# Top-32 attention and a routed expert layer on one core: part of the scores computed ahead and kept in DRAM, and a row-sum step given to ScalarE

## The chip, the core and the metric

The kernel runs on one core of a Trainium2 chip. The engines named below are those of the profile: PE is TensorE (matrix products; PEld is its weight load), DVE is VectorE, ACT is ScalarE, POOL is GpSimd, and SP is the engine that issues most of the DMAs. The metric is the device time of one execution in microseconds (us); the number given for a kernel is the median of its runs.

## The reference

What is computed, cut to what matters:

```python
# q, k, v: (8 batches, 8 heads, 576 rows, 64), fp32
scores = scale * (q @ k.T)                        # 576 x 576 for each head
kth    = the 32nd largest score of each row
attn   = softmax of the scores >= kth, all others 0, divided by (row sum + 1e-9)
x      = heads of (attn @ v) side by side         # 4608 tokens x 512

logits = x @ w_gate                               # 8 experts
e      = argmax(logits); gate = its softmax probability
out    = gate * (relu(x @ w1[e]) @ w2[e])         # w1: 512 x 1024, w2: 1024 x 512 for each expert
```

## The kernel before, in words

**Units and turns.** Two heads of one batch make a *unit*: the 128 partitions of its `qkb` tile hold both heads' 64 dimensions. A batch has four units, worked on in two pairs. A 576-row score matrix is cut into four tiles of 128 rows and a tail of 64 rows. `groups` (L229) orders the work of a pair: four groups of two tiles (tile i of both heads) of the first unit, one group of tails (both units), four groups of the second unit. That is 9 *turns* for a pair, 18 for a batch, 144 in all. Batches are counted from 1 here, as in the title; the code counts them from 0.

**One turn** (`loop`, L909) does these things for group i, and each belongs to a fixed engine, in an order written out by hand for PE, ACT and DVE:

- `products` (L263, matmuls L276): PE computes scores into PSUM tiles `sc`, four turns ahead. The four matmuls of a group take the two heads, that is, the lower and the upper 64 partitions, in alternation.
- `scores` (L279, L283): ACT copies them to SBUF, tile `s`, three turns ahead (`AHEAD`). There are four buffers of `s`.
- `fold` and `fold_on` (L290 to L300): DVE folds the scores of group i+1 by maximum and minimum. `search` (L317 to L354): DVE finds the 32nd largest of each row by rounds of MAX8 and MATCH_REPLACE8 (L329 to L345). Its last result goes to `low`, by ACT (L354).
- `depths` (ACT, L370), `less` (POOL, L379) and `weights` (ACT, L387, exponentials with the row sums added up into `z`) make the attention weights `w`.
- `transposed` (PE L398 to L411, ACT L404 to L419) turns the weights of group i-1.

**Endings.** When a unit's tiles are done, `ending` (L804) multiplies by v (`outputs`, L421: PE L432, ACT L434), turns the result back (PE L443, ACT L450), and makes divisors from the row sums (`divisors`, L452). These steps are spread over the following turns: each `yield` of `ending` names a place of the turn (`"products"`, `"relu"`, `"small"` ...) at which `at_place` resumes it. Small DVE steps are put into a list `aside`; `tick` (L304) issues one of them between two instructions of the search. `divisors` consists of three such steps on DVE: the sum plus 1e-9 (L454), its reciprocal (L456), and a copy of 64 values of the last column to other partitions (L458). POOL then multiplies by the divisors (`logits` L466, `rows` L479).

**Expert blocks.** Rows are scattered in DRAM by expert (L546). A *block* of 128 rows of one expert takes 4 MB of weights, two DMAs by SP (L635, L637), and is computed on PE in 16 pieces (`block`, L674: L688 and L703). `pieces` (L773) puts some of them into each turn by a credit that grows by a fixed `rate`; from the 14th turn of a batch on (`FIRST`) the rate is set by the number of blocks that became known with the batch before. The number of pieces put into the turns does not depend on any time. What is left runs after the last turn.

**Queues.** SP carries out its DMAs strictly in the order in which the scheduler placed them: an instruction that waits for a buffer holds all behind it. `load_unit` (L141) brings `qkb` (two buffers), `load_values` (L245) brings v, and the pool `wp` has two buffers each for `w1` and `w2`. POOL's order is placed by the scheduler too.

The functions that the diff touches, and what calls them:

Of the kernel before, what the change touches and what calls it, by code (L numbers as in the profile page):

```python
# [9 lines left out]
F32 = mybir.dt.float32  # L10
I32 = mybir.dt.int32
AF = mybir.ActivationFunctionType
# [9 lines left out]
EPS = 1e-9  # L22
# [13 lines left out]
def kernel(  # L36
# [6 lines left out]
    moe_w2: bass.AP,  # L43
    out: bass.AP,
):

# [36 lines left out]
    nc = tc.nc  # L83
# [6 lines left out]
    NC = 4  # L90
# [103 lines left out]
    for n in range(2):  # L194
        t = const.tile([P, S if n else KC * P], F32, name=f"oT{n}")
        if not n:
            nc.gpsimd.memset(t[:, S:], 0.0)
        oT_of.append(t)
        t = const.tile([P, NT + 1], F32, name=f"rz{n}")
        nc.gpsimd.memset(t, 0.0)  # L200
        rz_of.append(t)
    wT = const.tile([P, NC, 2, S + ST], F32, name="wT")
    wTt = const.tile([P, S + ST], F32, name="wTt")
# [75 lines left out]
    def scores(got):  # L279

        s = k.att.tile([P, 2, 2, HF], F32, name="s", bufs=2 if k.exact else 4)
        return s, [
            lambda m=m, ps=ps: nc.scalar.copy(s[:, m, :, :], ps[:, :, 0:HF]) for m, ps in enumerate(got)  # L283
        ]
# [166 lines left out]

    def divisors(n):  # L452
        rz = rz_of[n.u % 2]
        nc.vector.tensor_scalar_add(rz[:, 0:NT], n.z, EPS)  # L454
        yield
        nc.vector.reciprocal(rz[:, 0:NT], rz[:, 0:NT])  # L456
        yield
        nc.vector.tensor_copy(rz[0:ST, NT:NT + 1], rz[ST:P, NT - 1:NT])  # L458
        yield

    def logits(n, lg):
# [269 lines left out]
    ON_CHIP = 3  # L731
    KEEP = 3 * PIECES
    BETWEEN = 2

    with fast:
        units = [(b, u) for b in range(B) for u in range(U)]
# [67 lines left out]
        def ending(b, u):  # L804

            nonlocal left
            n = unit[b * U + u]
            if u == 0:
                x_of[b] = k.xp.tile([P, KC, XW], F32, name="x")
                in_turn(token_ids(x_of[b][:, :, Dm + 1].bitcast(I32), b))  # L810
                lg_of[b] = k.small.tile([P, KC, E], F32, name="lg")
            x, lg = x_of[b], lg_of[b]
            out_steps = outputs(n, x)
            yield "products"
            next(out_steps)
            if u % 2 == 0:
                yield "relu"
                next(out_steps)
            yield "small"
            div = divisors(n)  # L820
            aside.append(div)
            if u % 2:
                yield "relu"
                next(out_steps)
            yield "products"
            next(out_steps)
            if b * U + u + 2 < len(units):
                load_values(unit[b * U + u + 2])
            yield "relu"
            next(out_steps)  # L830
            yield "products"
            next(out_steps)
            yield "relu"
            next(out_steps, None)
            yield "rows"
            through(div)
            logits(n, lg)
            rows(n, x)
            if u < U - 1:
                return  # L840
            yield "small"
            r = choice(lg)
            aside.append(r.steps)
            yield "weights"
            yield "turn"
            through(r.steps)
            nc.scalar.activation(lg, lg, AF.Exp)
            yield "products"
            ranks(r)
            yield "small"  # L850
            steps = places(r, x)
# [12 lines left out]
            new = LAST - SURE if b == B - 1 else new_of[b]  # L864
            if new:
                slot_i = slot_last if b == B - 1 else k.small.tile([1, 2, NSLOT], I32, name="slot_i")
                steps = table(slot_i, new, b == B - 1)
                aside.append(steps)
                yield "weights"
                yield "pool"  # L870
                yield "weights"
                yield "pool"
                through(steps)
                coming.extend((slot_i[0:1, 0, j:j + 1], slot_i[0:1, 1, j:j + 1]) for j in range(new))
            if b == B - 1:
                spare.extend(coming[ALWAYS - SURE:])
                del coming[ALWAYS - SURE:]
                assert len(loaded) == 2 and not waiting
                fill_up()
                coming[0:0] = [(firsts[0][0], ready)] + [(expert, (piece,)) for expert, piece in firsts[1:]]  # L880
                scatter(0)
# [9 lines left out]

        got_of, s_of, f_of, w_of = {}, {}, {}, {}

        def tiles_of(i):
            b, g = work[i]
            return [(unit[b * U + u], tile) for u, tile in g]
# [3 lines left out]

        def multiply(i):
            tiles = tiles_of(i)
            got_of[i] = products(tiles)
            n, tile = tiles[0]
            more = n.b * U + n.u + 2
            if tile == (NC - 1 if n.u % 2 else 2 * NC) and more < len(units):
                unit.append(load_unit(*units[more]))

        def loop():  # L909
            nonlocal credit, rate, clock  # L910
            for i in range(min(AHEAD, len(work))):
                multiply(i)
                s_of[i], steps = scores(got_of.pop(i))
                for step in steps:
                    step()
            multiply(AHEAD)
            f_of[0] = fold(s_of[0])
            fold_on(f_of[0])
            for i, (b, g) in enumerate(work):
                tiles = tiles_of(i)  # L920
                u, tile = g[0]
                if tile == 0 and u % 2 == 0:
                    open_unit(tiles[0][0])
                if tails(tiles):
                    open_unit(tiles[1][0])

                then = lambda: None
                if i + 1 < len(work):
                    f_of[i + 1] = fold(s_of[i + 1])
                    then = lambda: fold_on(f_of[i + 1])  # L930
                low, nbias, doubts = search(tiles, s_of[i], f_of.pop(i), then)
                at_place("small")
                w_of[i] = depths(s_of[i], low)
                less(s_of.pop(i), w_of[i])
                doubts()
                put_stores()
                scatter(1)
                at_place("pool")
                at_place("relu")
                at_place("rows")  # L940
                at = i % per_batch
                if at == FIRST and b:
                    rate = new_of[b - 1] * PIECES / (U * NT)
                credit += rate * len(g)
                room = left
                if b == B - 1 and at >= ARRIVED:
                    room -= KEEP
                    credit = room / (len(work) - i)
                share = {0: 0.5, 1: 1.2, 2: 1.6, 3: 0.5, 2 * NC: 1.4}[tile]
                now = max(0, min(int(credit * share + 0.5), room))  # L950
                credit -= now
                clock = i
                if i + AHEAD < len(work):
                    s_of[i + AHEAD], steps = scores(got_of.pop(i + AHEAD))
                    for step in steps:
                        step()
                evacuate()
                at_place("turn")
                turns = turning(i - 1) if i else iter(())
                next(turns, None)  # L960
                part = min(BETWEEN, now - now // 2)
                rest = pieces(part)
                next(turns, None)
                rest = pieces(now - now // 2 - part + rest)
                weights(tiles, w_of[i], nbias)
                next(turns, None)
                evacuate()
                if i + AHEAD + 1 < len(work):
                    multiply(i + AHEAD + 1)
                if tile == NC - 1:  # L970
                    end = ending(b, u)
                    late.append([end, next(end)])
                at_place("products")
                at_place("weights")
                credit = min(credit + pieces(now // 2 + rest), 6 * rate)
# [147 lines left out]
```

## Time and profile before

| what | value |
|---|---|
| median of 3 runs (lowest, highest) | 1375.64 us (1375.47, 1375.88) |
| the profiled execution's own time | 1374.78 us |
| its span, first to last instruction | 1372.9 us |
| PE busy over the span | 1235.4 us (90%) |
| DVE busy | 1092.9 us (80%) |
| ACT busy | 919.6 us (67%) |
| POOL busy | 646.9 us (47%) |
| DMA moved | 231.68 MB, mean 169 GB/s |

How to read it: a share of the span is a mean over two very different stages. Up to about 1100 us the attention runs, with expert blocks put into its turns; after that only expert blocks run. Which engine sets the pace has to be read stage by stage. A row of the groups gives line, engine and operation, then `out<-in` with shapes and the count, then busy time and mean duration, then the idle time of the engine in front of the instructions. A row of the view by stretches gives the stretch, its length, the busy time of PE, PEld, DVE, ACT and POOL (each with the number of instructions), PE's granted clock as a share of full speed, the DMA share and GB/s.

### The profile page before, as it was taken

The numbers are of one execution on the slowest core, as the hardware profiler recorded it, in microseconds if no ns is written. First come the engines' busy times: TensorE is split into PE (matmuls) and PEld (weight loads), VectorE is DVE, ScalarE is ACT, GpSimd is POOL, SyncE is SP. The second block draws the span as 40 slices with busy tenths as digits, with TensorE's granted clock in tenths as the row PEclk, the third lists the DMA queues.
The fourth block names the chain that finished last, engine by engine and source line by source line (L and its number), as shares of the span: only waits on it lengthen the run. The fifth ranks groups of instructions, "written<-read, shape, count | busy, mean of one in ns | idle before, by whom it ended". The sixth has DMA issues, their size and how long they took to land. (4 is left out here: it accounts for less than half of the span.)

```text
span 1372.9 us, 24487 instructions
## 1 busy us (share of the span) xinstructions
PE 1235.4 (90%) x7666; PEld 839.2 (61%) x7666; DVE 1092.9 (80%) x4655; ACT 919.6 (67%) x2049; POOL 646.9 (47%) x805
## 2 busy tenths in 40 slices
PE   5676777677899999999999999999999999999995
PEld 3344444344466666666766666767676676776773
DVE  8999999999999999999999999999999820000000
ACT  4788777778788888888777788887777821111110
POOL 3454547546645666466555655575556521000000
PEclk9888788877899999999999999999999999999998
DMA  2000011001483367427654474358542859999880
GB/s 82 29 29 29 28 36 55 29 29 36 154 299 130 111 204 286 133 78 248 249 169 172 153 279 155 114 177 301 186 167 77 305 182 356 389 323 329 304 321 18
DMA packets 102220, 231.68 MB, mean 169 GB/s; under 512 B 5182, under 2 KB 25918, under 8 KB 102080
## 3 DMA queue, kind: packets, MB, share of 16 engines
q1 hardware_dynamic: 95328, 209.76, 43.6%
q0 software_dynamic: 6464, 19.97, 4.0%
q8 instruction: 62, 1.02, 0.3%
q14 instruction: 78, 0.64, 0.1%
q10 hardware_dynamic: 288, 0.30, 0.1%
HBM read 208.72 MB, written 22.33 MB: 168 GB/s over the span
## 5 line engine op out<-in xcount | busy, mean ns | idle before, releaser
L379 POOL TENSOR_TENSOR w<-s,w 128x576 f32<-128x576 f32 x288 | 407.4, 1435 | 449.4 <-ACT w L370 449.2
L688 PE MATMUL ph<-xTs,w 128*128 128x128 f32 x2560 | 308.6, 276 | 6.3 <-ACT xTs L665 6.0
L688 PEld LDWEIGHTS ph<-xTs,w 128*128 128x128 f32 x2560 | 297.4, 192 | 26.9 <-issue 19.6
L703 PE MATMUL py<-w,hT 128*128 128x512 f32 x640 | 292.2, 596 | 0.0
L338 DVE MAX8 tops<-scr 128x8 f32<-128x168 f32 x864 | 250.0, 323 | 0.1
L276 PE MATMUL sc<-qkb 64*128 64x288 f32 (+1 forms) x1280 | 223.6, 475 | 9.3 <-ACT s L283 5.2
L387 ACT ACTIVATE w<-w,nbias 128x576 f32<-128x576 f32 x288 | 224.8, 799 | 2.2 <-POOL w L379 2.0
L370 ACT ACTIVATE w<-s,low 128x576 f32<-128x576 f32 x288 | 207.7, 768 | 4.7
L398 PE MATMUL wTm<-turn,w 128*128 128x128 f32 x1152 | 174.0, 292 | 35.2 <-ACT xl L450 24.0
L398 PEld LDWEIGHTS wTm<-turn,w 128*128 128x128 f32 x1152 | 135.3, 148 | 96.1 <-issue 35.8
L1002 DVE CAST any_i<-pd 1x1 int32<-1x1 f32 x1 | 0.1, 145 | 236.6 <-PE pd L1000 236.6
L703 PEld LDWEIGHTS py<-w,hT 128*128 128x128 f32 x640 | 114.5, 190 | 117.6 <-issue 116.5
L345 DVE MATCH_REPLACE8 scr<-tops,scr 128x168 f32<-128x168 f32 x576 | 178.9, 317 | 0.0
L283 ACT COPY s<-sc 128x576 f32<-128x576 f32 x288 | 169.9, 645 | 11.0 <-PE sc L276 10.4
L404 ACT COPY wT<-wTm 128x512 f32<-128x512 f32 x256 | 139.8, 610 | 38.8 <-PE wTm L398 38.6
L276 PEld LDWEIGHTS sc<-qkb 64*128 64x128 f32 (+1 forms) x1280 | 118.7, 196 | 72.8 <-issue 25.7
L432 PE MATMUL po<-wT,vb 128*64 128x288 f32 x1024 | 155.0, 450 | 0.4 <-ACT wTt L419 0.4
L709 POOL DMA_INDIRECT out_dram<-y,xg x40 | 40.6, 1014 | 212.5 <-ACT y L717 199.8
L329 DVE MAX8 few<-l 128x8 f32<-128x288 f32 x288 | 129.2, 448 | 0.0
L432 PEld LDWEIGHTS po<-wT,vb 128*64 128x64 f32 x1024 | 74.7, 151 | 78.0 <-issue 28.5
L693 ACT ACTIVATE hT<-ph 128x512 f32<-128x512 f32 x80 | 48.7, 609 | 109.2 <-PE ph L688 109.2
L290 DVE TENSOR_TENSOR h<-s 128x576 f32<-128x576 f32 x144 | 114.9, 798 | 3.8 <-ACT s L283 3.8
(116 smaller groups left out, 1432.1 us busy)
## 6 DMA issues: line engine op xcount, KB each, us to landing
w<-in_moe_w_dram SPq DMA_DIRECT2D x80, 2048.0 KB, 9.5
qkb<-in_qk_dram SPq DMA_DIRECT2D x31, 608.0 KB, 4.3
xg<-x_rows SPq DMA_DIRECT2D x40, 257.0 KB, 10.1
vb<-in_v_dram SPq DMA_DIRECT2D x32, 320.0 KB, 3.3
x_rows<-blank SPq DMA_DIRECT2D x5, 257.0 KB, 15.6
x_rows<-blank POOLq DMA_DIRECT2D x4, 257.0 KB, 8.6
x_rows<-x,posi POOLq DMA_INDIRECT x40, 3.3
out_dram<-y,xg POOLq DMA_INDIRECT x40, 6.1
```

Source lines behind the costliest of these rows:

```text
L276: nc.tensor.matmul(ps[rows, j, 0:HF], n.q[d, cols], n.k[d, keys], start=True, stop=True)
L283: lambda m=m, ps=ps: nc.scalar.copy(s[:, m, :, :], ps[:, :, 0:HF]) for m, ps in enumerate(got)
L338: nc.vector.max(out=tops[:, m, r * 8:(r + 1) * 8], in_=src[m])
L345: nc.vector.match_replace(out=scr[:, m, :], in_to_replace=tops[:, m, r * 8:(r + 1) * 8], in_values=src[m], imm_value=NEG,)
L370: nc.scalar.activation(w[:, m, :], s[:, m, :, :].rearrange("p j k -> p (j k)"), AF.Relu, scale=-STEEP, bias=low[:, m:m + 1],)
L379: k.last_pool = in_turn(nc.gpsimd.tensor_tensor(w[:, m, :], s[:, m, :, :].rearrange("p j k -> p (j k)"), w[:, m, :], op=ALU.subtract)).ins
L387: nc.scalar.activation(w[:, m, :], w[:, m, :], AF.Exp, scale=scale, bias=nbias[:, m:m + 1], accum_out=n.z[:, c:c + 1])
L398: nc.tensor.transpose(pm[:, c * P:(c + 1) * P], w[:, m, first:first + P], ident)
L404: nc.scalar.copy(wT[:, :, m, q], pm4)
L432: nc.tensor.matmul(po[r, 0:HF], n.v[:, c, r], rhs, start=(c == 0), stop=(c == KC - 1))
L688: nc.tensor.matmul(ph[:, f, :], n.w1[:, 0, dt, fc * P:(fc + 1) * P], n.xT[:, dt, :], start=(dt == 0), stop=(dt == DT - 1),)
L703: nc.tensor.matmul(py, hT[:, f, :], n.w2[:, 0, f, :], start=(f == 0), stop=(f == FT - 1))
```

## The change

Four edits:

1. Batches 4 to 8 have their second unit's four full groups marked as `early` (5 x 4 = 20 groups). A generator `earlier` computes their scores during the turns 2 to 41, one half of a group (one head's tile) in each: two matmuls by PE into a `sc` tile and one copy by ACT into a buffer borrowed from the weight pool `wp`, which also holds the unit's `qk`, loaded for this by SP. After every second half SP stores the group, 576 KB, in DRAM.
2. Where such a group's turn comes, there are no matmuls and no ACT copies for it: `fetch_scores` has SP load the stored scores straight into an `s` buffer, at the place at which ACT would have copied them.
3. In `divisors` the addition and the move of the 64 values are now two ACT instructions that read `z`; DVE keeps one reciprocal over 10 columns instead of 9. Because all 128 rows of the tenth column are now inverted, `rz` starts as 1.0.
4. In `ending` the place of `divisors` moves: the two ACT instructions go out at the place `"relu"`, for the second unit of a pair behind the copy of its first output half (old L434).

```diff
-        nc.gpsimd.memset(t, 0.0)
+        nc.gpsimd.memset(t, 1.0)
         rz_of.append(t)
...
     def divisors(n):
         rz = rz_of[n.u % 2]
-        nc.vector.tensor_scalar_add(rz[:, 0:NT], n.z, EPS)
+        nc.scalar.activation(rz[:, 0:NT], n.z, AF.Copy, bias=EPS)
+        nc.scalar.activation(rz[0:ST, NT:NT + 1], n.z[ST:P, NT - 1:NT], AF.Copy, bias=EPS)
         yield
-        nc.vector.reciprocal(rz[:, 0:NT], rz[:, 0:NT])
-        yield
-        nc.vector.tensor_copy(rz[0:ST, NT:NT + 1], rz[ST:P, NT - 1:NT])
+        nc.vector.reciprocal(rz[:, 0:NT + 1], rz[:, 0:NT + 1])
         yield
...
+    EARLY_FOR = 3
...
             yield "products"
             next(out_steps)
+            yield "relu"
+            next(out_steps)
             if u % 2 == 0:
                 yield "relu"
-                next(out_steps)
-            yield "small"
             div = divisors(n)
+            next(div)
             aside.append(div)
-            if u % 2:
-                yield "relu"
-                next(out_steps)
             yield "products"
...
+        early = {}
+        for i, (b, g) in enumerate(work):
+            if b >= EARLY_FOR and g[0][0] == 1 and g[0][1] < NC:
+                early[i] = dram.tile([P, 2, 2, HF], F32, name=f"early{i}")
+
+        def earlier():
+
+            todo = sorted(early)
+            own = []
+
+            def open_own(p):
+                if p * NC >= len(todo):
+                    return
+                room = k.wp.tile([P, 1, DT, F], F32, name="w1") if p % 2 == 0 else k.wp.tile(
+                    [P, 1, FT, Dm], F32, name="w2")
+                room = room.rearrange("p a b c -> p (a b c)")
+                nc.sync.dma_start(room[:, 0:2 * S + ST], qk[work[todo[p * NC]][0], 1, :, :])
+                own.append(room)
+
+            open_own(0)
+            for at, i in enumerate(todo):
+                if at % NC == 0:
+                    open_own(at // NC + 1)
+                room = own[at // NC]
+                first = 2 * S + ST + (at % 2) * 2 * S
+                put = room[:, first:first + 2 * S].rearrange("p (m j k) -> p m j k", m=2, j=2)
+                cols = slice((at % NC) * P, (at % NC + 1) * P)
+                for m in range(2):
+                    ps = k.ps_s.tile([P, 2, SM], F32, name="sc")
+                    d = slice(m * D, (m + 1) * D)
+                    for j in range(2):
+                        keys = slice(S + (0 if m else ST) + j * HF, S + (0 if m else ST) + (j + 1) * HF)
+                        nc.tensor.matmul(ps[:, j, 0:HF], room[d, cols], room[d, keys], start=True, stop=True)
+                    nc.scalar.copy(put[:, m, :, :], ps[:, :, 0:HF])
+                    if m:
+                        nc.sync.dma_start(early[i], put)
+                    yield
...
-            got_of[i] = products(tiles)
+            got_of[i] = None if i in early else products(tiles)
...
+        def fetch_scores(i):
+            got = got_of.pop(i)
+            if got is None:
+                s_of[i] = k.att.tile([P, 2, 2, HF], F32, name="s", bufs=4)
+                nc.sync.dma_start(s_of[i], early[i])
+                return
+            s_of[i], steps = scores(got)
+            for step in steps:
+                step()
...
                 if i + AHEAD < len(work):
-                    s_of[i + AHEAD], steps = scores(got_of.pop(i + AHEAD))
-                    for step in steps:
-                        step()
+                    fetch_scores(i + AHEAD)
                 evacuate()
                 at_place("turn")
                 turns = turning(i - 1) if i else iter(())
                 next(turns, None)
+                if i:
+                    next(ahead_of, None)
                 part = min(BETWEEN, now - now // 2)
```

The order of the instructions on the engines, taken from both built kernels: POOL's is the same, the order of the weight loads on SP is the same, the pieces of the expert blocks keep their places, and the `qkb` load of the fourth unit of the batches 4 to 8 moves forward on SP to stand right behind that of the third. In the batches 4, 5 and 7 the four loads of stored scores stand on SP as: two behind the third unit's load of v, then a `w1` load, two more, then a `w2` load. In the batches 6 and 8 they stand: `w1` load, two, `w2` load, a load of rows, two.

More of the change, by code (lines that the diff above doesn't have):

```diff
@@ L907, in multiply @@
                 unit.append(load_unit(*units[more]))
+        def fetch_scores(i):
[7 more added lines that the diff above has]
+                step()
         def loop():
             nonlocal credit, rate, clock
+            ahead_of = earlier()
             for i in range(min(AHEAD, len(work))):
                 multiply(i)
-                s_of[i], steps = scores(got_of.pop(i))
-                for step in steps:
-                    step()
+                fetch_scores(i)
             multiply(AHEAD)
@@ L953, in loop @@
                 if i + AHEAD < len(work):
-                    s_of[i + AHEAD], steps = scores(got_of.pop(i + AHEAD))
-                    for step in steps:
-                        step()
+                    fetch_scores(i + AHEAD)
                 evacuate()
```

## The prediction

> **What bounds the kernel now.** I read the busy slices first, then the view by stretches cut at the batches, then groups, then single turns on the timeline. The slices:
>
> ```profile
> PE   5676777677899999999999999999999999999995
> DVE  8999999999999999999999999999999820000000
> ...
> PEclk9888788877899999999999999999999999999998
> ```
>
> DVE is full for 31 slices and stops in the 33rd; PE fills up from the 12th slice and stays full to the end. So there are two stages, one set by DVE up to about 1101 us, one by PE alone behind it. Batches 1, 4 and 6 and the last stage by stretches (lengths, then PE, PEld, DVE, ACT, POOL):
>
> ```profile
> 0.00:132.00 132.00, 90.72 (x463) 53.49 (x463) 125.35 (x541) 93.82 (x208) 58.33 (x90) 0.87 0.14 44
> ...
> 395.40:528.80 133.40, 130.71 (x874) 90.35 (x874) 133.24 (x581) 111.69 (x252) 78.90 (x97) 1.00 0.52 182
> ...
> 663.70:808.10 144.40, 143.18 (x953) 99.58 (x952) 142.98 (x581) 113.31 (x255) 82.82 (x98) 1.00 0.55 194
> ...
> 1100.80:1345.00 244.20, 242.05 (x1420) 177.40 (x1417) 7.61 (x43) 41.85 (x74) 25.28 (x30) 1.00 0.87 310
> ```
>
> The reader is to see three things. In batch 1 PE has 41 us to spare, at a granted clock of 0.87. In batch 4 DVE is full and PE nearly. In batch 6 DVE executes the same 581 instructions and yet is "busy" 9.7 us longer: its instructions are stretched. The starts of the folds (L290) show it turn by turn: an undisturbed turn takes 7.02 us (499.47, 506.49, 513.51), but the turns 2, 5, 6 and 9 of batch 6 take 8.43, 8.54, 10.04 and 9.82. Batch 8 repeats this. What stretches them is seen on the timeline of DVE and POOL:
>
> ```profile
> 682.54 2.79 POOL L379 TENSOR_TENSOR w<-s,w 128x576 f32<-128x576 f32 x2 [2.44 <-ACT w L370]
> ...
> 683.18 0.80 DVE L454 TENSOR_SCALAR rz<-z 128x9 f32<-128x9 f32 x1
> 683.90 0.32 DVE L338 MAX8 tops<-scr 128x8 f32<-128x168 f32 x1
> 684.14 0.19 DVE L456 RECIPROCAL rz<-rz 128x9 f32<-128x9 f32 x1
> ...
> 686.16 0.45 DVE L298 TENSOR_TENSOR few<-h 128x288 f32<-128x288 f32 x1
> ```
>
> L379 is two instructions of 1.40 us, the second from 683.91. L454 ends with the first (683.98), while MAX8 and the reciprocal run unhindered beside the second. In all 11 stretched L454 the end is that of an L379; stretched L298 and L290 end with an L379 or an L479. In late batches ACT and POOL come late because PE is full, L379 then slides under DVE's instructions, and DVE pays.
>
> The last stage holds the fixed rest of expert blocks on PE. It starts where the attention ends, so a microsecond saved before is one saved at the end.
>
> **Part 1: the divisors.** The rows:
>
> ```profile
> L454 DVE TENSOR_SCALAR rz<-z 128x9 f32<-128x9 f32 x32 | 14.8, 464 | 0.8 <-ACT w L387 0.8
> L456 DVE RECIPROCAL rz<-rz 128x9 f32<-128x9 f32 x32 | 6.2, 194 | 0.0
> L458 DVE COPY rz<-rz 64x1 f32<-64x1 f32 x32 | 4.8, 149 | 0.9
> ```
>
> Instructions overlap, so I take the price from turns: one with these three steps and no other takes 7.46 to 7.48 us, 0.45 more than 7.02. Of that the reciprocal, which stays, is 0.12 (518.52 to the next start, 518.63). **Saved: 32 x 0.33 = 10.6 us.** Besides, L454's stretch goes: 14.8 - 32 x 0.174 (its median) = **9.2 us**. Next late there would be L298, about 2.0 us behind: in the four units where the second L379 is then running, it ends 0.1, 0.6, 0.1 and 0.6 us after L298's new start; the new wait below covers this, so I don't add it.
>
> The new wait: the reciprocal now waits for two ACT instructions. Their rows are near: `low` (128x2) 194 to 268 ns, `run` (128x8) 155; so 0.3 to 0.5 for both, I take 0.35. On ACT they stand behind `depths`, and for odd units behind the copy L434, which waits for PE. Taking the end of the ACT instruction in front from this trace, plus 0.35, against the start of L454: 22 of the 31 units in the loop come in time, seven late units don't: 1.5 us twice, 0.8 four times, 0.2 once, together 6.3. In the example above L434 ends at 684.34, so the reciprocal would start at 684.7 instead of 683.2. Two early units have 0.25 and 0.31 to spare and become up to 0.7 late each with part 2; I take **-8 us** in all, bounds 0 (the lateness goes with part 3) and -14 (each late unit twice as late). Behind the reciprocal the whole search waits. The two instructions themselves, 64 x 0.2 = 13 us, lie in ACT's waits for `tops` (88.7 us in 74 waits); without those they would delay `low`.
>
> The Trainium skill, page "ScalarE: Activation LUTs", section "Rules for kernel authors", advises VectorE for additions, as up to about three times faster per element. By that rule this part would save nothing, and the sum would be without its 10.6 + 9.2; by the rows, nine elements cost either engine under 0.2 us unhindered, and it counts which of the two is full.
>
> **Part 2: the scores computed ahead.** 40 halves in the turns 2 to 41. PE: the group row says
>
> ```profile
> L276 PE MATMUL sc<-qkb 64*128 64x288 f32 (+1 forms) x1280 | 223.6, 475 | 9.3 <-ACT s L283 5.2
> ...
> L283 ACT COPY s<-sc 128x576 f32<-128x576 f32 x288 | 169.9, 645 | 11.0 <-PE sc L276 10.4
> ```
>
> and a whole group takes 1.24 us on the timeline (x8), since its matmuls go to both halves of the array in turn. An early half goes to one half only: 0.62 us if that cost nothing, 1.0 from the L703 row's spacing (0.43 for 512 columns, so 0.24 for 288, x4), twice that at half clock. It lies in the time in which PE idles, 41 us in batch 1, 36 and 30 in the next two. ACT: one copy per turn, 0.6 us. An early turn shows what hides it:
>
> ```profile
> 67.44 0.20 ACT L354 ACTIVATE low<-tops 128x2 f32<-128x2 f32 x1 [1.27 <-DVE tops L338]
> ...
> 70.77 1.10 ACT L404 COPY wT<-wTm 128x512 f32<-128x512 f32 x2
> 71.72 0.82 ACT L387 ACTIVATE w<-w,nbias 128x576 f32<-128x576 f32 x1
> ...
> 74.57 0.20 ACT L354 ACTIVATE low<-tops 128x2 f32<-128x2 f32 x1 [1.03 <-DVE tops L338]
> ```
>
> The copy goes in front of L387; ACT waits 1.0 to 1.8 us for `tops` in most early turns. Where it waits only 0.2 (four turns of batches 1 and 2), `low` comes 0.4 late, and L379 ends 1.8 us before L298 elsewhere, so nothing collides. In turns with L450, PE runs late and at times at half clock; there a collision of up to 1.4 us can come, at nine endings. **-3 us**, bounds 0 and -12. SP's extra five loads and 20 stores use a queue that waits most of that time (DMA share 0.14).
>
> **Part 3: the turns relieved.** In batches 4 to 8, 20 turns lose 1.24 us of PE and 20 lose two ACT copies, 1.2 us. In batches 4, 5 and 7 DVE sets the pace and gains nothing by it. In batches 6 and 8 the relief falls on the turns 2 to 5, and the stretches in the turns 2, 5, 6 and 9 (L454 apart) add up to 5.3 us, each under an L379 or L479 that PE made late. I take 4.5 of each, **+9 us**; bounds 0 and 2 x 7.5. Stretches from turn 12 on stay, as `low` is back in time at turn 11 even now. A fall of the clock would cost PE only the slack it gained; no row shows a clock between 77% and 98% busy.
>
> The loads: the nearest row is `qkb`, 608 KB, 3.4/4.3/11.9 us to landing (min, median, max). A stored `s` is asked for when POOL's L379 of four turns before lets go of the buffer, some 4.5 us into a turn, and needed 1.4 turns later, by 14.0: about 5 us of slack. The tightest are the first ones in batches 6 and 8, behind a `w1` load: SP issues that at 692.73, the `s` load at 693.3; `w1` lands 7.8 us after its issue at the least, 0.58 MB more at that pace is 2.2 us, the fourth unit's `qkb`, now in front, another 0 to 2.3: 702.7 to 705, and the fold is due at 702.9. **-2 us** for both, bounds 0 and -8. Weight loads move by under 2 us and are used at least three turns later.
>
> **Sum.** 10.6 + 9.2 - 8 - 3 + 9 - 2 = 15.8 us. The profiled execution took 1374.78 (span 1372.9), so 1359.0; the median lies 0.9 above it: **1360 us**.
>
> **Rivals.**
> *PE's relief counts in full.* PE is 98% busy from 400 us on; if it, and not DVE, holds those batches, 20 x 1.24 = 25 us go: 1350. For it: batches 6 and 8 take 11 us more than batch 4. Against: batch 4's turns are exactly 7.02.
> *The new waits eat the gain.* The reciprocal's waits at their far end (-14), no relief in batches 6 and 8, loads late (-5): 10.6 + 9.2 - 14 - 3 + 0 - 5 = -2, that is 1378 at worst; with half the relief kept, 1370 to 1373. For it: the late units sit where ACT is late already.
> *ScalarE becomes the bound of the first 41 turns* (slower). If the early matmuls, at half clock 2 us in front of the copy on PE, make ACT wait until its 1.0 to 1.8 us of slack are gone, each turn grows by the copy, 40 x 0.65 = 26 us: 15 - 26 makes 1386. It decides as soon as `low` starts over 1.8 us after the search's end. Against: the granted clock is the higher the fuller PE is (0.82 to 0.87 in batches 1 to 3, 1.00 behind them).
> *The edits cancel*: 1375.
>
> **How the numbers follow.** Chances: forecast 0.56, PE in full 0.15, waits eat 0.12 (of it 0.03 unmeasurable), ScalarE bound 0.14, cancel 0.03. A difference under 0.2%, 2.8 us, can't be told from none. Faster 0.56 + 0.15 + 0.09 = 0.80, same 0.06, slower 0.14. The range runs from 1346, below the PE rival, to 1377 in the second rival; it leaves out the slower case and little else.
>
> **What would show it.** L454's and L458's lines gone from DVE, the reciprocal's mean over 0.3 us in late units; batch 1 to 3 within 2 us of 132.0, 131.2, 132.2; batch 6 near 138 instead of 144.4; the last stage still 244 us long. Wrong if early L354 waits vanish, if L290 waits for a DMA by more than 8 us in sum, or if batch 6 keeps its length.

## The result and the profile after

| | before | after |
|---|---|---|
| median of 4 runs (lowest, highest) | 1375.56 us (1373.84, 1375.88) | 1374.78 us (1373.84, 1377.32) |
| ratio, 95% interval | | 1.000 (0.998 to 1.002) |
| span of the profiled execution | 1372.9 us | 1373.3 us |
| start of the last fold (group 144) | 1081.5 us | 1081.5 us |

The change makes no difference that can be measured. A gain of 15.8 us was forecast. It is missing before the last fold already. From there to the end both kernels take the same (291.4 and 291.8 us).

The busy slices of the changed kernel's page, the rows that were shown of before:

```profile
PE   6988898888799999999999999999999999999995
DVE  8999999999999999999989999999899820000000
...
PEclk9698979898799999999999999999999999999998
```

PE's first ten slices rise from 5 to 7 tenths to 8 and 9 in most: the early scores. The 21st and the 29th slice of DVE fall below 9, in batches 6 and 8, which they did not before. The same stretches as before, cut at the new starts of the batches (batch 1, 4, 6, the last stage; columns: stretch, length, PE, PEld, DVE, ACT, POOL, granted clock, DMA share, GB/s):

```profile
0.00:133.90 133.90, 112.32 (x505) 66.23 (x505) 126.47 (x534) 100.76 (x223) 60.02 (x90) 0.86 0.28 97
401.80:534.00 132.20, 126.32 (x845) 87.69 (x843) 132.05 (x572) 109.41 (x253) 82.40 (x97) 1.00 0.58 202
666.70:811.80 145.10, 140.95 (x924) 99.24 (x924) 140.59 (x571) 112.31 (x259) 87.09 (x101) 0.99 0.60 213
1100.80:1345.00 244.20, 242.42 (x1424) 177.52 (x1421) 7.83 (x44) 42.28 (x77) 25.02 (x30) 1.00 0.86 310
```

Batch 1 has 21.6 us more of PE and is 1.9 longer (132.00 to 133.90). Batch 4 is 1.2 shorter. Batch 6 lost ten DVE instructions and 2 us of PE and is 0.7 *longer*; DVE now idles 4.5 us in it. The groups of the steps that were changed:

```profile
L287 ACT COPY s<-sc 128x576 f32<-128x576 f32 x248 | 145.5, 641 | 10.0 <-PE sc L280 10.0
L294 DVE TENSOR_TENSOR h<-s 128x576 f32<-128x576 f32 x144 | 115.4, 801 | 10.0 <-ACT s L287 5.7 <-DMA s<-early 4.3
...
L928 PE MATMUL sc<-w 64*128 64x288 f32 x160 | 52.6, 451 | 20.8 <-ACT s L287 20.8
...
L929 ACT COPY w<-sc 128x576 f32<-128x576 f32 x40 | 26.5, 664 | 3.5 <-PE sc L928 3.5
L458 ACT ACTIVATE rz<-z 128x9 f32<-128x9 f32 x32 | 6.7, 208 | 0.0
L461 DVE RECIPROCAL rz<-rz 128x10 f32<-128x10 f32 x32 | 6.5, 204 | 15.0 <-ACT rz L459 14.5
L459 ACT ACTIVATE rz<-z 64x1 f32<-64x1 f32 x32 | 6.4, 202 | 0.4
```

Three waits are new: the reciprocal's for ACT (14.5 us), the folds' for loads (4.3 us, two of them), and 20.8 us in which PE stands at the early matmuls L928 until ACT has emptied a score buffer.

**Batch by batch.** All else goes by this table: the time from one batch's first fold to the next one's (batch 8 to its 18th fold), in one profiled execution of each kernel. Executions of the same kernel differ by up to 4 us in all, so a difference of 1 us in one cell means little, and a pattern over several kernels counts.

| kernel | 1 | 2 | 3 | 4 | 5 | 6 | 7 | 8 | last fold starts |
|---|---|---|---|---|---|---|---|---|---|
| before | 124.3 | 131.3 | 132.1 | 133.4 | 134.9 | 144.4 | 136.2 | 137.2 | 1081.5 |
| after | 126.1 | 134.0 | 133.9 | 132.2 | 132.7 | 145.1 | 132.7 | 137.0 | 1081.5 |
| e1_divisors_only | 123.6 | 131.0 | 130.6 | 133.4 | 134.8 | 146.2 | 134.8 | 138.2 | 1080.5 |
| e2_early_only | 125.5 | 133.1 | 132.3 | 133.3 | 134.4 | 143.3 | 135.1 | 134.5 | 1079.5 |
| e3_pairs | 125.2 | 131.7 | 130.8 | 132.3 | 132.7 | 143.5 | 132.7 | 135.9 | 1072.7 |
| e4_act_fetch | 127.1 | 133.9 | 133.9 | 132.2 | 132.7 | 145.1 | 132.7 | 137.2 | 1082.7 |
| f2_pairs_later | 124.5 | 130.8 | 132.0 | 131.8 | 132.3 | 145.1 | 132.3 | 136.8 | 1073.6 |
| f3_pairs_three | 124.2 | 129.2 | 131.2 | 132.1 | 132.7 | 146.2 | 132.7 | 138.2 | 1074.4 |
| f5_other_turns | 124.9 | 132.5 | 135.7 | 144.9 | 132.3 | 159.0 | 132.9 | 151.2 | 1121.3 |
| f6_no_first | 124.2 | 130.7 | 130.8 | 132.3 | 132.3 | 143.0 | 132.3 | 134.8 | 1068.5 |
| f7_third_unit | 123.1 | 132.2 | 132.4 | 131.8 | 132.3 | 144.4 | 132.3 | 136.1 | 1072.4 |
| g1_before_light | 124.6 | 131.0 | 132.2 | 132.2 | 132.2 | 136.5 | 132.3 | 129.5 | 1058.5 |
| g2_divisors_light | 123.2 | 129.4 | 130.6 | 130.7 | 130.7 | 133.9 | 130.7 | 126.9 | 1044.5 |
| g3_after_light | 127.2 | 134.0 | 133.8 | 130.7 | 130.7 | 134.3 | 130.7 | 126.1 | 1055.5 |

After against before: +1.8, +2.7, +1.8, -1.2, -2.2, +0.7, -3.5, -0.2. So it is a sum of losses and gains near zero, not a change without effect. (In code and rows, old L290 is now L294, L298 is L302, L300 is L304, L379 is L383.)

### The profile page after: what moved, and what is told of

The parts are those of the page before. It is cut to its first block, busy times and chain, and to the rows that moved or that the text cites. A ratio compares the mean times of both kernels' runs of the same rounds, so it can differ in the third digit from the quotient of the medians.

```text
span 1373.3 us, 24583 instructions
## 1 busy us (share of the span) xinstructions
PE 1271.8 (93%) x7666; PEld 863.0 (63%) x7666; DVE 1079.3 (79%) x4591; ACT 930.7 (68%) x2113; POOL 665.5 (48%) x805
## 5 line engine op out<-in xcount | busy, mean ns | idle before, releaser
L383 POOL TENSOR_TENSOR w<-s,w 128x576 f32<-128x576 f32 x288 | 408.7, 1440 | 433.3 <-ACT w L374 433.2
L342 DVE MAX8 tops<-scr 128x8 f32<-128x168 f32 x864 | 245.8, 316 | 0.0
L280 PE MATMUL sc<-qkb 64*128 64x288 f32 (+1 forms) x1120 | 213.6, 471 | 9.5 <-ACT s L287 5.2
L402 PE MATMUL wTm<-turn,w 128*128 128x128 f32 x1152 | 170.1, 287 | 34.7 <-ACT xl L454 14.6
L402 PEld LDWEIGHTS wTm<-turn,w 128*128 128x128 f32 x1152 | 131.5, 145 | 94.6 <-issue 37.3
L280 PEld LDWEIGHTS sc<-qkb 64*128 64x128 f32 (+1 forms) x1120 | 114.4, 192 | 72.7 <-issue 20.1
L287 ACT COPY s<-sc 128x576 f32<-128x576 f32 x248 | 145.5, 641 | 10.0 <-PE sc L280 10.0
L294 DVE TENSOR_TENSOR h<-s 128x576 f32<-128x576 f32 x144 | 115.4, 801 | 10.0 <-ACT s L287 5.7
```

Source lines behind the costliest of these rows:

```text
L280: nc.tensor.matmul(ps[rows, j, 0:HF], n.q[d, cols], n.k[d, keys], start=True, stop=True)
L342: nc.vector.max(out=tops[:, m, r * 8:(r + 1) * 8], in_=src[m])
L383: k.last_pool = in_turn(nc.gpsimd.tensor_tensor(w[:, m, :], s[:, m, :, :].rearrange("p j k -> p (j k)"), w[:, m, :], op=ALU.subtract)).ins
L402: nc.tensor.transpose(pm[:, c * P:(c + 1) * P], w[:, m, first:first + P], ident)
```

## Experiments

### One part at a time

Theory A, my first: the divisors' saving is real, and the stored scores give it back. Four runs test it and its rivals, which their expectations name.

**e1_divisors_only**: nothing is computed early.

```diff
-    EARLY_FOR = 3
+    EARLY_FOR = 8
```

> No unit is computed ahead; only the divisors are changed. Theory A (the divisors' saving is real, the stored scores give it back): batches 1 to 3 shorter by 1.3 us each than before (124.3, 131.3, 132.1), batches 4, 5, 7 by 1.2, 2.2, 3.4 as in the changed kernel, batches 6 and 8 by 1.8 each (1.3 for the two DVE steps and 2.9 for the stretched L454, less 2.4 of waits of the reciprocal); in sum 14 us, about 1361 to 1362. Theory B (PE holds the pace from 400 us on, so what DVE saves comes back as waits): only the 4 us of batches 1 to 3, about 1371. Theory C (the change of the divisors is worth nothing at all): 1375.

**e2_early_only**: early scores kept, `divisors` and its place in `ending` as before.

```diff
-        nc.scalar.activation(rz[:, 0:NT], n.z, AF.Copy, bias=EPS)
-        nc.scalar.activation(rz[0:ST, NT:NT + 1], n.z[ST:P, NT - 1:NT], AF.Copy, bias=EPS)
+        nc.vector.tensor_scalar_add(rz[:, 0:NT], n.z, EPS)
...
```

> The scores are computed ahead and fetched, the divisors stay as before. Theory A: batches 1 to 3 longer by 3.0, 4.2, 3.0 us than before, batches 4, 5 and 7 unchanged, batches 6 and 8 longer by the late load, 2.2 us each, less what relief there is (0 to 2): +10 to +15 us, 1386 to 1390. Theory B: batches 6 and 8 shorter by 5 us each for the 4 x 1.24 us that PE no longer does there: about +1, 1376. Theory C: 1375.

**e3_pairs**: an early step computes a whole group, its matmuls alternating between the heads, in every second turn.

```diff
-                for m in range(2):
-                    ps = k.ps_s.tile([P, 2, SM], F32, name="sc")
...
+                yield
+                both = [k.ps_s.tile([P, 2, SM], F32, name="sc") for m in range(2)]
+                for j in range(2):
+                    for m, ps in enumerate(both):
```

> The changed kernel, with both halves of a group in every second turn, their matmuls on the two halves of the array in alternation. Theory A in the form that PE's time decides (an early half takes 1.24 us on one half of the array, a whole group the same 1.24 on both): 25 us of PE work less in batches 1 to 3, those batches shorter by 3 to 6 us in sum than in the changed kernel, about 1370. Theory A in the form that ACT's copies decide (two of them, 1.2 us, now in one turn): as long or longer, 1375 to 1380. Theories B and C: 1375.

**e4_act_fetch**: the stored scores are asked for by ACT instead of SP.

```diff
-                nc.sync.dma_start(s_of[i], early[i])
+                nc.scalar.dma_start(s_of[i], early[i])
```

> The changed kernel, with the stored scores asked for by ACT instead of SP, so that they don't stand behind a weight load in SP's queue. Theory A: the two gaps of 2.2 us before the fold in batches 6 and 8 go, 1371 if nothing takes their place; ACT pays 0.4 us for each issue, in turns where it no longer copies. Rival: the load shares the DMA engines with the weight load whichever queue asks, and stays 1 to 2 us late: 1374. Theory B: no change, 1375.

Measured, against 1375.71 of before: e1 1374.34 us (0.9986, 0.9976 to 0.9997), e2 1372.87 (0.9978, 0.9968 to 0.9989), e3 1367.64 (0.9946, 0.9928 to 0.9963), e4 1376.48 (1.0003, 0.9994 to 1.0013).

**Theory A falls.** The divisors alone are worth 1.4 us, not 11.8. Theory B does not fit either: it gave e1 4 us in batches 1 to 3, and they are 2.5 shorter. Theory C's 1375 fits e1, but the next section shows that the divisors are not worthless. e2 lies below what A, B and C expected of it. In e1 the DVE steps went as foreseen; what they left free was taken by others. The folds of before, and then of e1 (columns: count, then busy time and mean ns):

```profile
L290 DVE TENSOR_TENSOR h<-s 128x576 f32<-128x576 f32 x144 | 114.9, 798 | 3.8 <-ACT s L283 3.8
...
L300 DVE TENSOR_TENSOR hl<-h 128x288 f32<-128x288 f32 x144 | 67.5, 469 | 0.0
...
L454 DVE TENSOR_SCALAR rz<-z 128x9 f32<-128x9 f32 x32 | 14.8, 464 | 0.8 <-ACT w L387 0.8
```

```profile
L294 DVE TENSOR_TENSOR h<-s 128x576 f32<-128x576 f32 x144 | 119.6, 830 | 5.8 <-ACT s L287 5.8
...
L304 DVE TENSOR_TENSOR hl<-h 128x288 f32<-128x288 f32 x144 | 71.3, 495 | 0.0
...
L461 DVE RECIPROCAL rz<-rz 128x10 f32<-128x10 f32 x32 | 6.7, 208 | 11.2 <-ACT rz L459 10.9
```

L454's stretch is gone, but L294 and L304 are 4.7 and 3.8 us longer for the same count (L302, 76.9 us against the 78.5 of old L298, is 1.6 shorter), and the reciprocal waits 10.9 us (6.0 of it in the last unit, where the wait for `lg` shrank from 10.0 to 5.2). In batches 4 and 5 the table shows no gain at all: 133.4 and 134.8 against 133.4 and 134.9. How that happens is seen on the timeline of the changed kernel in batch 6 (DVE and POOL):

```profile
680.11 3.00 POOL L383 TENSOR_TENSOR w<-s,w 128x576 f32<-128x576 f32 x2 [2.60 <-ACT w L374]
...
680.62 1.22 DVE L302 TENSOR_TENSOR few<-h 128x288 f32<-128x288 f32 x1
681.76 1.66 DVE L304 TENSOR_TENSOR hl<-h 128x288 f32<-128x288 f32 x1
```

Undisturbed, both take some 0.45. With the divisors' steps gone DVE reaches L302 sooner, while the two L383 still run; L302 is held until the first ends, L304 until the second (it ends 0.31 us behind it), 1.99 us together. The page "SBUF — State Buffer" of the Trainium skill, section "Who interferes with whom", says that a VectorE instruction with two SBUF inputs and a GpSimd instruction that reads SBUF exclude each other, and that whichever starts second is blocked until the first ends. These rows agree.

**Where PE and DVE are equally full, both divisors and relief are needed.** In batches 4, 5 and 7 e1 gives 0, -0.1 and -1.4, e2 -0.1, -0.5 and -1.1, and both together -1.2, -2.2 and -3.5. (In batch 7 the two parts alone already make most of it.)

**The early turns cost more with the new divisors.** Batches 1 to 3: e2 against before +3.2 in sum, after against e1 +8.8. PE in batch 1 of the changed kernel:

```profile
77.40 1.17 PE L402 MATMUL wTm<-turn,w 128*128 128x128 f32 x8
80.01 1.23 PE L928 MATMUL sc<-w 64*128 64x288 f32 x4 [1.44 <-ACT s L287]
81.18 0.33 PE L415 MATMUL wTl<-turn,w 128*128 128x128 f32 x1
81.44 1.86 PE L280 MATMUL sc<-qkb 64*128 64x288 f32 x8
```

The early half takes 1.23 us, as long as a whole group of eight in its own turn from batch 4 on (1.24; the one shown, in batch 1, takes 1.86). It first waits 1.44 for a score buffer, and everything behind it on PE waits too. e3 takes about a third off both: the 160 early matmuls (L928, in e3 L929) fall from 52.6 us to 37.0 and their waits from 20.8 to 13.5, batches 1 to 3 become 6.3 us shorter and the kernel 7.1. For a group that is 2.6 us in halves and 1.85 in pairs, against the 1.24 that its own turn is spared. The page "TensorEngine Tiling (Array Packing)", section "When to Use Tiling", advises to pack two matmuls by rows where the contraction is 64 long; the early halves undid that packing, and the two sums of busy time above, a factor of 1.4, agree with the page in direction.

e4 does not help (1371 was expected if SP's order were the cause): with ACT asking, five folds wait for loads, 5.7 us, instead of two, 4.3. SP's order alone is not what makes them late.

### PE with room to spare

Theory D, formed from these: from batch 4 on DVE and PE set the pace together, so DVE's saved steps come back as stretches and waits. Then, with PE lightened, the same divisors must bring what was forecast.

**g1_before_light** and **g2_divisors_light**: before, and e1, with half of the expert blocks' first product left out.

```diff
-                for dt in range(DT):
+                for dt in range(DT // 2):
```

> The kernel before with half of the L688 matmuls left out (the sum over two of four parts only), so that PE has some 4 us less per block. Theory A has fallen with the divisors alone, which moved nothing. Theory D: in batches 4 to 8 the turn is a loop of PE, ACT, POOL and DVE with DVE and PE both full, so that what one of them saves comes back as stretched and waiting DVE instructions. Then without PE's load batches 4 to 8 take 131 to 132 us each instead of 133.4, 134.9, 144.4, 136.2, with hardly a stretch. Rival E (the stretches come from where ACT and POOL stand in the turn, not from PE): batches 6 and 8 stay above 140. In both the last stage shrinks by 4 us for each of its blocks, some 60 us, so compare the batches.

> The same half of the matmuls left out, with the changed divisors and nothing computed ahead; to be read against the kernel before with the same left out. Theory D: now DVE alone sets the pace, and the two saved DVE steps show in every batch, 1.3 us each, 10 us in sum. Rival F (the reciprocal's wait for ACT eats the saving wherever it stands): under 3 us in sum, with gaps before the reciprocal in most units.

Measured, in two runs of each: 1313.73 and 1300.54 us against 1374.95 of before (0.9551, 0.9532 to 0.9570; 0.9456, 0.9437 to 0.9474). **The divisors save 13.2 us here**, 13.9 at the last fold, and in every batch (1.4 to 2.6). Batch 4 of g1, then of g2:

```profile
395.80:528.00 132.20, 120.81 (x748) 76.93 (x747) 132.04 (x581) 111.34 (x252) 79.31 (x97) 0.99 0.52 185
```

```profile
391.60:522.20 130.60, 120.42 (x748) 77.02 (x747) 130.60 (x572) 112.99 (x260) 79.07 (x97) 0.99 0.52 186
```

PE is busy 121 of 132 us instead of 130.7 of 133.4, DVE is full, and nine instructions less are 1.6 us less. The rows of g1 that were stretched before:

```profile
L290 DVE TENSOR_TENSOR h<-s 128x576 f32<-128x576 f32 x144 | 110.5, 767 | 1.9 <-ACT s L283 1.9
...
L298 DVE TENSOR_TENSOR few<-h 128x288 f32<-128x288 f32 x144 | 70.0, 486 | 0.0
...
L454 DVE TENSOR_SCALAR rz<-z 128x9 f32<-128x9 f32 x32 | 5.8, 182 | 1.3 <-ACT w L387 1.3
```

L454's mean is 182 ns, not 464, though nothing on DVE was changed. So L454's stretch comes from PE's load. That it goes by way of ACT and of L379 (now L383), which come late and hold DVE, is read from the timelines and not tested apart. In batch 6 PE's load is not the whole cause: g1 takes 136.5 us there, more than theory D's 132 and less than rival E's 140, and of the 12.2 us by which DVE's instructions exceeded their lines' medians, 5.7 are left. The last stage became 38 us shorter, not some 60. In g2 only the last unit's reciprocal waits (6.2 us, once).

**g3_after_light**: the changed kernel with the same half left out.

> The changed kernel whole, with half of the matmuls of the expert blocks' first product left out (dt runs over DT // 2; its output is not the reference's), to stand beside g1_before_light (last fold at 1058.5 us) and g2_divisors_light (1044.5). Theory D (the stored scores relieve only PE, so they gain nothing where PE has room, and the early turns cost what they cost in full): the last fold at 1050 to 1055 us, batches 4, 5 and 7 within 0.5 us of 130.7, batch 6 within 1 us of 133.9. Rival (the stored scores help by ScalarE's two copies less as well): batch 6 and 8 together shorter than 133.9 and 126.9 by more than 2 us.

Measured: 1310.26 us (0.9526, 0.9510 to 0.9542), last fold at 1055.5, 11.0 after g2's and 0.5 outside theory D's bounds. Batches 4, 5 and 7 are g2's to a tenth, 6 and 8 within 0.8. **With room on PE the stored scores gain nothing, and all of their cost stands in batches 1 to 3** (+4.0, +4.6, +3.2). That ACT has two copies less in 20 turns is worth nothing that shows.

### Cheaper early turns, and relief elsewhere

**f2_pairs_later**: e3, and the reciprocal is put into `aside` one place later, so that ACT has time.

```diff
             next(div)
-            aside.append(div)
             yield "products"
...
             yield "relu"
+            aside.append(div)
             next(out_steps)
```

> The changed kernel with both halves of a group in every second turn, as in the run before, and the reciprocal handed to the search one turn later, so that it doesn't wait for ACT. Theory D: what the waits cost in batches 1 to 3 (2 to 4 us in the changed kernel) goes; in batches 6 and 8 the 2.3 us of each come back as stretches: 1364 to 1366. Rival F: all of the 4 + 2 x 2.3 us go, 1358 to 1360.

**f3_pairs_three**: e3, but nothing stored for batches 6 and 8.

```diff
-            if b >= EARLY_FOR and g[0][0] == 1 and g[0][1] < NC:
+            if b in (3, 4, 6) and g[0][0] == 1 and g[0][1] < NC:
```

> The changed kernel with pairs, but computed ahead for the batches 4, 5 and 7 alone (12 groups instead of 20, turns 2 to 25). If the relief in batches 6 and 8 is worth nothing because the late load takes it back: batches 6 and 8 as long as with the divisors alone (146.2, 138.2 to the last fold) or shorter by up to 1, batch 2 and 3 without the early work shorter by 1 to 2: 1367 to 1369. If the late load (2.2 us) is all that is wrong there: 145.1 and 137.0 become 144 and 136, 1364.

Measured, with 1374.95 for before: f2 1365.01 us (0.9920, 0.9903 to 0.9936), f3 1368.06 (0.9953, 0.9936 to 0.9969). Both are in the range of the first theory of their expectations. f2's reciprocal waits for ACT in the last unit only. f2's waits of DVE, from the view of waits (total, times, longest):

```profile
DVE rz L461 <- ACT rz L459: 6.0, 1, 6.0
...
DVE h L294 <- DMA s<-early: 4.6, 2, 2.3
DVE h L294 <- ACT s L287: 4.2, 5, 1.6
```

Yet batch 6 is 145.1 as in the changed kernel: DVE's waits in it fell from 5.5 to 3.4 us, and its stretches (again the time over the lines' medians) rose from about 11 to 13.2. In f3 batches 6 and 8 are e1's (146.2, 138.2), so relief in the turns 2 to 5 was worth 1 to 3 us in each (1.1 and 1.4 in f2, 2.7 and 2.3 in e3), not the 4.5 that I took.

**f5_other_turns**: f2, but for batches 6 and 8 the third and fourth units are stored, 28 groups in all. The early routine is made general for that; the choice is:

```diff
-            if b >= EARLY_FOR and g[0][0] == 1 and g[0][1] < NC:
+            if (b, g[0][0]) in ((3, 1), (4, 1), (5, 2), (5, 3), (6, 1), (7, 2), (7, 3)) and g[0][1] < NC:
```

> The kernel f2_pairs_later (1365.0 us, last fold at 1073.6) with other groups stored: the second units of batches 4, 5 and 7 as there, but of batches 6 and 8 the third and the fourth unit, so that PE is relieved in the turns 6 to 9 and 11 to 14 of these, 28 groups instead of 20. Theory D (in batches 6 and 8 both DVE and PE are full, and relief pays where it falls late enough to meet the stretched turns): the stretches there fall from 13 us to 7 to 9, batches 6 and 8 take 139 to 142 instead of 145.1, the time 1355 to 1361 us. Rival (what PE gains by relief is lost whenever its turns come, since the waits for ScalarE or for the load take its place): batches 6 and 8 stay within 1.5 us of 145, the time within 2 us of 1365. Second rival (PE's hours before batch 4 have no room for four groups more): the sum of the first three batches grows by over 3 us.

Measured: 1413.49 us (1.0277, 1.0260 to 1.0294), worse than any case foreseen. Its waits of DVE, and SP's timeline before the longest:

```profile
DVE h L294 <- DMA s<-early: 41.4, 4, 17.6
DVE h L294 <- ACT s L287: 8.2, 10, 1.6
```

```profile
794.99 0.40 SPq L638 DMA_DIRECT2D w<-in_moe_w_dram  x1
795.63 0.38 SPq L640 DMA_DIRECT2D w<-in_moe_w_dram  x1
...
799.37 0.37 SPq L638 DMA_DIRECT2D w<-in_moe_w_dram  x1
802.64 0.71 SPq L640 DMA_DIRECT2D w<-in_moe_w_dram  x1
803.48 9.36 SPq L961 DMA_DIRECT2D s<-early  x1
```

Four folds wait 41.4 us. Of these the waits in turn 17 of batches 6 and 8 (fourth unit) make 17.6 and 16.9. Before the longest the load is asked for behind four weight loads of 2 MB within 8 us, and the issue alone takes 9.36 us instead of 0.33. The other two (0.8 and 6.1 us) are in batch 4, into which the early work of 28 groups reaches: its last store goes out at 444.9 us. The second rival shows as well: batches 1 to 3 are 5.8 us longer than in f2. This run therefore doesn't tell whether relief in later turns pays.

**f6_no_first**: f2 without the first stored group of batches 6 and 8, whose load is late.

```diff
-            if b >= EARLY_FOR and g[0][0] == 1 and g[0][1] < NC:
+            if b >= EARLY_FOR and g[0][0] == 1 and g[0][1] < NC and (b in (3, 4, 6) or g[0][1]):
```

> The kernel f2_pairs_later with the first stored group of batches 6 and 8 computed in place again, 18 groups instead of 20. If the late load of that group's scores (a gap of 2.1 us in front of its fold in each of the two batches) is what these batches lose, they become 1.5 to 2 us shorter each and the time falls by 3 to 4 us, to about 1361.5. If the gap only lets POOL and ScalarE catch up, and its time comes back as stretches, batches 6 and 8 stay within 0.7 us of 145.1.

Measured: 1364.27 us (0.9924, 0.9907 to 0.9941), the fastest of the kernels that compute everything. The waits for loads are gone and batches 6 and 8 are 2.1 and 2.0 shorter than f2's in the profiles, but the median is only 0.7 lower, the runs overlap (1363.1 to 1365.8, 1363.2 to 1367.1), and the ratios to before, 0.9920 and 0.9924, are no different; e3 has that wait and 143.5 in batch 6. What the late load costs is not settled between 0 and 4 us.

**f7_third_unit**: f2 with the third unit of batches 6 and 8 stored instead of the second.

```diff
-            if b >= EARLY_FOR and g[0][0] == 1 and g[0][1] < NC:
+            if (b, g[0][0]) in ((3, 1), (4, 1), (5, 2), (6, 1), (7, 2)) and g[0][1] < NC:
```

> The kernel f2_pairs_later (1365.0 us, last fold at 1073.6) with the third unit of batches 6 and 8 stored instead of the second, 20 groups as there, so that PE is relieved in the turns 6 to 9 of these two. In f5_other_turns the loads of the third unit came in time; only those of the fourth stood behind three weight loads. Theory D (both engines are full in batches 6 and 8, and relief pays where it is in front of stretched turns): no wait of a fold for a load in these batches, stretches of 9 to 10 us instead of 13.2 and 12.0, batch 6 at 140.5 to 142.5 instead of 145.1 and batch 8 as much shorter, last fold at 1066 to 1069, the time 1358 to 1361 us. Rival (relief is lost wherever it falls): batch 6 within 1 us of 145.1 and the time within 2 us of 1365.

Measured: 1368.75 us (0.9950, 0.9933 to 0.9966, against 1376.05). No fold waits for a load, and batch 6 takes 144.4. The rival held on batch 6 (its time, within 2 us of 1365, is missed by 1.8: the stretch behind the last fold took 293.6 us here and 291.8 in f2), and theory D's figures (batch 6 at 140.5 to 142.5, 1358 to 1361 us) fell: four relieved turns change little there, in both places tried, while g1's load, lighter in every turn, makes batch 6 7.9 us shorter. Batch 6 of f7:

```profile
659.60:804.00 144.40, 139.85 (x925) 97.55 (x925) 143.16 (x572) 112.51 (x258) 88.23 (x101) 1.00 0.61 213
```

PE is still busy 139.9 of 144.4 us. The stretches lie in 13 of its 18 turns, most of their time in turns that are not relieved. Why these turns do not draw on the room gained before them is open.

## Why the prediction was wrong

The same terms, as the runs measure them at the last fold:

| step | forecast | measured | from |
|---|---|---|---|
| divisors (10.6 + 9.2 - 8) | +11.8 | +1.2 | e1 against before, batches 1 to 8 |
| early turns | -3 | -8.8 | after against e1, batches 1 to 3 |
| relief in batches 4, 5, 7 | 0 | +5.4 | after against e1 |
| relief in 6 and 8, loads (9 - 2) | +7 | +2.3 | after against e1 |
| sum | +15.8 | +0.1 | |

The split is one of two orders. Taken the other way at the last fold, the stored scores alone gain 2.0 us (e2 against before) and the divisors on top of them lose 2.0 (after against e2); the two parts do not simply add up.

- **Failed: part 1**, as the prediction put it: "Saved: 32 x 0.33 = 10.6 us", "L454's stretch goes: 14.8 - 32 x 0.174 (its median) = 9.2 us". The price of the steps was not too high: with room on PE the same divisors save 13.2 us (g1 and g2), 2.6 more than the 10.6. What failed is the path: the saving was charged in full in batches where PE is full as well, and there it came back as stretches of other instructions and as waits, so that 1.2 us are left of 11.8. The prediction saw that PE was 98% busy and dismissed it with "batch 4's turns are exactly 7.02". Undisturbed turns show that DVE sets the pace of *those* turns; they don't show that PE could follow a faster DVE.
- **Failed with it: the stretch as a saving.** L454's stretch under L379 (now L383) was not a cost of L454's own: it went in g1, where L454 stayed and PE had less to do. Take away the instruction that is held, and the next with two inputs is held (L294, L302, L304). "Next late there would be L298 ... the new wait below covers this, so I don't add it" was the sentence that had it in hand.
- **Near, in part by luck: the wait of the reciprocal.** Forecast 8 us; measured 14.5 in sum, of which 6.0 in the last unit replace 4.8 of an older wait, so about 9.7. But of the seven late units (6.3 us) four waited, 4.5 us, all in batches 6 and 8, and three early ones waited 3.9, up to 2.7 instead of 0.7. It was to show as a mean above 0.3 us; it shows as idle time in front, while the mean stays at 204 ns. The two ACT steps took 0.21 and 0.20 us, where the prediction read "under 0.2". The factor of three that it names stands on its page for bf16; in fp32 nine elements took 0.17 us on DVE (L454's median) and 0.21 on ACT.
- **Failed: part 2's size.** "0.62 us if that cost nothing, 1.0 from the L703 row's spacing": an early half took 1.23 us in the median and 1.31 on average, and it holds what is queued behind it on PE while it waits for a `sc` buffer, a wait that the prediction did not list. ACT's side was right: its waits for `tops` in the first 400 us fall from 51.4 us in e1 to 24.4, the 26.5 us of the copies, and do not vanish. The prediction's "the granted clock is the higher the fuller PE is" does not hold within these batches: PE's share in batch 1 rose from 69 to 84% and the clock went from 0.87 to 0.86.
- **Failed: part 3's place.** "In batches 4, 5 and 7 DVE sets the pace and gains nothing by it": with the divisors gone they gain 5.4. "I take 4.5 of each" in 6 and 8: 1.1 and 1.2. "Batch 6 near 138": 145.1, and the prediction named this as the sign that it was wrong.
- **Right:** the last stage keeps its length; the loads' waits, 2.17 us in front of one fold in each of batches 6 and 8, were foreseen in place and near the size, and what they cost in the end stays open.
- **The rivals.** "The new waits eat the gain" reached to 1378 and had the reciprocal's waits and the lost relief, but held the divisors' 19.8 for safe. "PE's relief counts in full" had the right reason, a full PE, and the wrong sum: with the divisors gone, relief gained 7.7 us of its 25 (5.4 and 2.3 above), and with room on PE none (g3). "The edits cancel" gave the number, with 3 in 100.

## What to carry to other kernels

Where two engines are both nearly full in a stage (here PE 98% and DVE 100% in batch 4), price a saving on one of them by what the other lets through; the same saving came through with PE at 91%. So look how long the second engine is busy in that stage, not whether some turns run at the first engine's pace. Of a saved instruction that was long only because it was blocked, count the undisturbed length: here whoever blocked it blocked the next. Work moved to a time with room still costs when it sits in an in-order queue with a wait in front of it, and when it loses the packing that it had in place: the same early scores cost 2.5 us instead of 8.8 in the first three batches once they were computed in pairs.

## What was not expected of the hardware

- L383 also holds very small DVE instructions: in batch 6 of the changed kernel L601 and L603, small sums and scans of one row, were 1.0 us longer than their median under it, each. MAX8, MATCH_REPLACE8 and the reciprocal were never held: in no run is one over 0.1 us above its median.
- In the relieved turns of batches 6 and 8 of the changed kernel the granted clock dips: from 719 to 726 us it is 0.76 with PE busy 5.78 of 7.00 us, while from 712 to 719 it is 1.00 with the same 5.78. One gap of 2.44 us (L402 waiting for ACT) ends at 720.22. From 997 to 1004 us it is 0.76 again. Before had 1.00 in every stretch of 7 us from batch 4 to the last fold. What the dip costs was not measured.
- The issue of one load by SP took 9.36 us with four weight loads of 2 MB just in front of it (f5); the median issue took 0.33.
